# A two-stage mixing and SoLU kernel: an earlier transform, another form of the last unit, and other queues for its transfers

## The chip, the cores and the metric

The kernel runs on one core of one Trainium2 chip. The metric is the device time of one execution in microseconds (us). Five engines work side by side, each through its own list of instructions in order: PE (matrix products), DVE (vector), ACT (scalar functions), POOL (general) and SP (it issues transfers only). Transfers that SP or ACT issue are called plain here; POOL can also issue indirect ones, in which a table of row numbers says where each row goes. "The clock" of the profile is the share of full speed that PE was granted.

## What is computed

```python
X = np.fft.fft(np.fft.fft(x, axis=1), axis=2).real     # x: (8, 3136, 256)
x = X.reshape(8 * 3136, 256)
h = x @ w_in                                           # (25088, 1024)
e = np.exp(h - h.max(-1, keepdims=True))
solu = h * e / (e.sum(-1, keepdims=True) + 1e-9)
mu, var = solu.mean(-1, keepdims=True), solu.var(-1, keepdims=True)
out = ((solu - mu) / np.sqrt(var + 1e-6) * g_ln) @ w_out   # (25088, 256)
```

A real part of a two-dimensional Fourier transform is followed by a feed-forward block with a softmax-weighted activation and a layer norm. Everything is float32.

## The kernel before, in words

The eight sequences are taken as four **pairs** (p = 0 to 3). The transform over the 3136 = 49 x 64 positions has two steps. The first (`transform1`, L176) works over 49; by symmetry only 25 of its outputs (k1 = 0 to 24) are needed. It goes through a pair in eight chunks c, two halves each, and its result passes through a scratch tensor `zd` in memory: `keep` (L215) writes it from SP, and `turn` (L218) reads it back on POOL in five parts. The second step (`transform2`, L226) gives 128 rows for one k1.

A **unit** is one pair and one k1: 100 units, number u = 25 p + k1. A unit with k1 > 0 also yields the mirrored output row block 49 - k1, so it has two **signs** (0 and 1), each a tile of 128 rows by 1024 features. Per unit: PE makes h (`up`, L259), DVE joins the halves (`even` L267, `join` L273), ACT exponentiates (`expo` L281), DVE multiplies (`product` L289), ACT takes sums of squares (`square` L296) and small statistics (`stats` L303), POOL takes a power (`power` L313). DVE then transposes in 32 by 32 blocks (`turn_both` L334), and transfers complete the transposition (`move_blocks` L358: 16 transfers, four source blocks i times four q). Two units form a **batch**, which has one tile `v` and one tile `uT`; the `uT` tile is used again two batches later.

The last product (2 x 128 rows by 1024, times `w_out`) comes five steps later. For two-signed units it takes the form of **seven block products** (`Down`, L403): POOL first makes four sums S0, S1, S3, S2 of blocks of `uT` (`sums`, L388), and PE then does seven products of four matmuls each, named in their order p1, p4, p5, p6, p2, p3, p7. ACT copies the first (`seed`, L425) and scales three intermediate results (`keep_p`, `keep_x`, `keep_c`), DVE ends the unit (`finish`, L455). p6 waits for `seed`, p3 for `keep_p`, p7 for `keep_x`. Other units use the plain form (`down`, L462, and `scale`, L471).

`store` (L475) writes a unit's rows: sign 0 by a plain transfer from SP, sign 1 by an indirect transfer from POOL with the row numbers in `idx`. Each indirect store waits until the one before it is complete.

**What sets the order.** It is written out by hand (L671), in one loop over steps i (L828 to L901). Step i takes unit i through its activation, unit i - 5 through its last product, and stores unit i - 6; POOL makes the sums for unit i - 4. The blocks of a batch are moved by SP in every even step (L876). The last batch, units 98 and 99, is moved apart from the others, in steps 100 and 101 (L897 to L901). The transform of the next pair runs inside the same steps: `SUMS` (L639) gives the step in which each chunk begins. At a = i - SUMS: a = 0 and 1 is the POOL sum of the mirrored halves (`add_mirror`, L128), a = 1 and 2 the fold on DVE and ACT, a = 3 and 4 the two halves of `transform1`, and at a = 2 the chunk two places on is loaded (`load`, L109: `xa` from SP, `xb` from POOL). `turn_parts` (L665) reads pair p's scratch at steps 25 p - 4, - 3, + 2, + 6 and + 11.

Every plain transfer, whichever engine issues it, raises one of eight counters, which are handed out in turn over SP and ACT together; before a transfer is issued, its counter has to show that its former user is complete.

Of the kernel before, what the change touches and what calls it, by code (L numbers as in the profile page):

```python
# [20 lines left out]
N1, N2 = 49, 64  # L21
NK = N1 // 2 + 1
# [4 lines left out]
NC = NH // CH  # L27
# [8 lines left out]
def kernel(  # L36
# [19 lines left out]
    nc = tc.nc  # L56
    B, S, D = x.shape
# [3 lines left out]
    NP = B // 2  # L61
# [35 lines left out]
    def result(i):  # L97

        return banks[i % 4]
# [159 lines left out]
    def up(t, c):  # L259

        ps = ps_h.tile([P, FF], FP32, tag=f"h{c}", name=f"ps_h{c}")
        for half in range(2):
            fs = slice(half * HW, (half + 1) * HW)
            nc.tensor.matmul(ps[:, fs], t.q[:, c * P : (c + 1) * P], Wi[:, c, fs], start=True, stop=True)  # L264
        return ps

    def even(t, ps):  # L267

        t.ev = fpool.tile([P, FF], FP32, tag="ev", name="ev", bufs=1)
        nc.vector.scalar_tensor_tensor(out=t.ev, in0=w_mid, scalar=t.r, in1=ps,  # L270
                                       op0=ALU.mult, op1=ALU.add)
# [24 lines left out]
    def square(t, s):  # L296

        if s == 0:
            t.ssq = small.tile([P, 2], FP32, tag="ssq", name="ssq")
        nc.scalar.activation(out=t.h[s], in_=t.u[s], func=ACT.Square, bias=t.usum[:, s : s + 1], scale=-float(FF),  # L300
                             accum_out=t.ssq[:, s : s + 1])

    def stats(t):  # L303

        n = slice(0, len(t.signs))
        es2, v = (small.tile([P, 2], FP32, tag=tag, name=tag) for tag in ("es2", "v"))
        nc.scalar.activation(out=es2[:, n], in_=t.esum[:, n], func=ACT.Square, bias=limits[:, 3:4], scale=1e-3)
        for s in t.signs:
            nc.scalar.activation(out=v[:, s : s + 1], in_=t.ssq[:, s : s + 1], func=ACT.Identity, bias=es2[:, s : s + 1],  # L309
                                 scale=float(FF) ** -3)  # L310
        t.v = v
# [46 lines left out]
    def move_blocks(batch, units, engines=(nc.sync,)):  # L358

        v = batch.v[:, units].rearrange("p w (c q n) s -> p q (w c) (n s)", q=4, n=32)  # L360
        uT = batch.uT[:, units].rearrange("p w c i m -> p i (w c) m")
        for i in range(4):
            for q in range(4):
                a, b = slice(32 * i, 32 * i + 32), slice(32 * q, 32 * q + 32)
                engines[i % len(engines)].dma_start(out=uT[b, i], in_=v[a, q])
# [22 lines left out]
    def sums(t, prv):  # L388

        A11, A12, A21, A22 = blocks(t)  # L390
        S = blocks_of(t)
        for j, a, b, op in ((0, A21, A22, ALU.add), (1, S[0], A11, ALU.subtract), (3, A12, S[1], ALU.subtract),
                            (2, A11, A21, ALU.subtract)):
            i = nc.gpsimd.tensor_tensor(out=S[j], in0=a, in1=b, op=op)  # L394
            if j == 0 and prv:
                behind(i, prv)
# [65 lines left out]
    def down(t, s, ps=None):  # L462

        uT = t.batch.uT[:, t.w].rearrange("p c i (n s) -> p c (i n) s", s=2)
        if ps is None:
            ps = result(1)[:, 0:D]
        for c in range(KF):
            nc.tensor.matmul(ps, uT[:, c, :, s], Wo[:, c, :], start=(c == 0), stop=(c == KF - 1))
        return ps

    def scale(t, s, ps):  # L471
        t.ot[s] = fpool.tile([P, D], FP32, tag="ot", name="ot", bufs=6)
        nc.scalar.mul(out=t.ot[s], in_=ps, mul=t.rs[:, s : s + 1])

    def store(t, s):  # L475

        if s:
            i = NP * NC + t.p * (NK - 1) + t.k1 - 1
            dma = nc.gpsimd.indirect_dma_start(  # L479
                out=out, out_offset=bass.IndirectOffsetOnAxis(ap=idx[:, i : i + 1], axis=0),  # L480
                in_=t.ot[s], in_offset=None)
        else:
            dma = nc.sync.dma_start(out=out_k[t.p, t.k1], in_=t.ot[s])

        tc.declare_no_dep(dma.ins, group=f"out{1 - s}", reason="other rows of the output")
        tc.add_to_no_dep_group(f"out{s}", dma.ins)

# [146 lines left out]

    SUMS = [None] + [[f + 2 * c for c in range(NC)] for f in (3, 28, 53)]  # L639

    def ahead(pr, i, work):

        for c in range(NC):
            a = i - SUMS[pr.p][c]
            if work == "load" and (i == (pr.p - 1) * NK and c < 2 or a == 2 and c + 2 < NC):
# [12 lines left out]
    def ahead_pe(pr, i):  # L658

        for c in range(NC):  # L660
            half = i - SUMS[pr.p][c] - 3
            if half in (0, 1):
# [8 lines left out]
    with tc.manual_schedule():  # L671
# [71 lines left out]
        units = [Unit(p, k1) for p in range(NP) for k1 in range(NK)]  # L743
# [10 lines left out]
        def second_transform(i):  # L754
            if i < len(units):
                t = units[i]
                take2(t, transform2(pairs[t.p], t.k1))
                spread(t)

        def enter(i):  # L760
            cur = units[i]
            if i % 2 == 0:
                batches.append(Batch(i >= whole))
            cur.batch, cur.w = batches[-1], i % 2
# [9 lines left out]
        def other_pairs(i, do, *a):  # L774
            cur = units[i]
            if cur.p + 1 < NP:
                do(pairs[cur.p + 1], i, *a)

        batches = []
        begin(0)  # L780
        for i in range(whole + 1):
            cur = units[i]
            prv = units[i - 1] if i else None
# [36 lines left out]

        def by_seven(i):

            return 0 <= i < len(units) - 1 and len(units[i].signs) == 2

# [1 line left out]
        for i in range(whole + 1, len(units) + lag + 1):  # L828
            cur = units[i] if i < len(units) else None
            prv = units[i - 1] if whole < i - 1 < len(units) else None  # L830
            old = units[i - lag] if i < len(units) + lag else None
            seven = by_seven(i - lag)
            kept = units[i - lag - 1] if i >= lag + 1 else None

            if kept:
                store(kept, 0)
            if cur:
                enter(i)
                even(cur, up(cur, 0))
                cur.odd = up(cur, 1)  # L840
                second_transform(i + 2)
            if seven:
                new = Down(old, fresh)
                fresh = False
                new.p1()
                new.seed()
            if prv:
                stats(prv)
            if seven:
                new.p4()  # L850
                new.p5()
                new.keep_p()
            elif old:
                plain = [(s, down(old, s, result(s + 1)[:, 0:D])) for s in old.signs]
            if cur:
                other_pairs(i, ahead_pe)
            if seven:
                new.p6()
                new.keep_x()
                new.p2()  # L860
                new.keep_c()
            elif old:
                for s, ps in plain:
                    scale(old, s, ps)
            if cur:
                for s in cur.signs:
                    join(cur, s)
            if seven:
                new.p3()
                new.p7()  # L870
                new.finish()
            if cur:
                other_pairs(i, ahead, "mirror")
            if by_seven(i + 1 - lag):
                sums(units[i + 1 - lag], prv)
            if i % 2 == 0 and whole < i - 1 < len(units) - 2:  # L876
                batches[i // 2 - 1].place()
                move_blocks(batches[i // 2 - 1], slice(0, 2))
            if prv:
                power(prv)  # L880
            if kept and 1 in kept.signs:
                store(kept, 1)
            if cur:
                other_pairs(i, ahead, "fold")
                for s in cur.signs:
                    expo(cur, s)
                for s in cur.signs:
                    product(cur, s)
                for s in cur.signs:
                    square(cur, s)  # L890
                turn_both(cur)
                if cur.p == 0 and i in (5, 8, 11):
                    turn(first, (i + 1) // 3)
                for pr in pairs[1:]:
                    turn_parts(pr, i - pr.p * NK)
                other_pairs(i, ahead, "load")
            if i in (len(units), len(units) + 1):  # L897
                w = i - len(units)
                if w == 0:
                    batches[-1].place()  # L900
                move_blocks(batches[-1], slice(w, w + 1), (nc.sync, nc.gpsimd) if w else (nc.sync,))  # L901


def _tables(B, S, D):
# [73 lines left out]
```

## Time and profile before

| what | us |
|---|---|
| median of three runs | 1170.49 (1167.22 to 1172.64) |
| the profiled execution, its own time | 1172.88 |
| its span, first to last instruction | 1171.0 |
| PE busy | 1115.0 (95%) |
| DVE busy | 1022.6 (87%) |
| POOL busy | 868.2 (74%) |
| ACT busy | 757.5 (65%) |
| mean granted clock | 0.993 |

The profile gives busy times by engine and by source line, who waited for whom, and a timeline with start, length and, in brackets, the idle time before an instruction and what ended it. `L394 POOL ... S<-uT` means line 394 on POOL, writing S from uT; x16 means that 16 records are merged in one row. In a row of SP or POOL that issues transfers the length is that of issuing, not of moving the data. One float32 matmul has two records.

### The profile page before, as it was taken

The page shows a single profiled execution, that of the slowest core. Times are in us where ns is not written, and L with a number is a line of the kernel's source. Part 1 is how long each engine was busy: PE and PEld are TensorE (multiplying, and loading weights), DVE is VectorE, ACT ScalarE, POOL GpSimd, SP SyncE. Part 2 cuts the span into 40 slices and gives each one's busy share as a digit, 9 for nine tenths or more (in the row PEclk, how much of TensorE's full clock was granted, in tenths as well). Part 3 has the DMA queues.
Part 4 walks back from the last instruction along what each step waited for, and adds up shares of the span by engine and source line. Part 5 has one row for each costly group of instructions (what it writes and reads, how often), then busy time and mean ns, then how long its engine had stood idle before and what let it go on. Part 6 is the DMA issues. An engine that isn't in the chain of part 4 may idle for free. (4 is left out here: it accounts for less than half of the span.)

```text
span 1171.0 us, 21594 instructions
## 1 busy us (share of the span) xinstructions
PE 1115.0 (95%) x7002; PEld 891.1 (76%) x7002; DVE 1022.6 (87%) x1428; ACT 757.5 (65%) x1721; POOL 868.2 (74%) x750
## 2 busy tenths in 40 slices
PE   2987999999999999999999999999999999999996
PEld 1555787787787777778878777878878788888886
DVE  7889989888999989999899999888898998998860
ACT  4566666667666666667666766676666666666651
POOL 3035888874998797887688889876598687777675
PEclk9999999999999989999999999999999999999998
DMA  9672798866897969886869797976596675956653
GB/s 240 197 190 45 168 186 186 196 144 145 157 182 155 186 149 174 170 174 143 161 133 202 156 190 164 205 174 144 134 168 154 130 161 113 165 120 134 137 120 93
DMA packets 458479, 185.75 MB, mean 159 GB/s; under 512 B 425750, under 2 KB 440350, under 8 KB 458368
## 3 DMA queue, kind: packets, MB, share of 16 engines
q1 hardware_dynamic: 444608, 146.22, 60.9%
q0 software_dynamic: 13760, 38.16, 12.5%
q8 instruction: 57, 0.93, 0.3%
q14 instruction: 54, 0.44, 0.1%
HBM read 44.78 MB, written 38.80 MB: 71 GB/s over the span
## 5 line engine op out<-in xcount | busy, mean ns | idle before, releaser
L264 PE MATMUL ps_h<-Wi,q 128*128 128x512 f32 x800 | 363.6, 596 | 11.4 <-DVE ev L270 5.9
L394 POOL TENSOR_TENSOR S<-uT 128x512 f32<-128x512 f32 x190 | 258.4, 1360 | 102.1 <-DMA r<-q 39.2
L300 ACT ACTIVATE h<-u,usum 128x1024 f32<-128x1024 f32 x196 | 225.2, 1149 | 155.8 <-DVE u L293 155.8
L401 PE MATMUL ps_m<-Ws,S 128*128 128x128 f32 x2280 | 297.3, 277 | 5.7 <-POOL S L394 3.3
L401 PEld LDWEIGHTS ps_m<-Ws,S 128*128 128x128 f32 x2280 | 280.0, 193 | 10.1 <-POOL S L394 3.7
L264 PEld LDWEIGHTS ps_h<-Wi,q 128*128 128x128 f32 x800 | 144.3, 191 | 160.0 <-issue 141.7
L293 DVE SCALAR_TENSOR_TENSOR u<-h,u 128x1024 f32<-128x1024 f32 x196 | 261.0, 1367 | 0.4 <-ACT u L286 0.3
L286 ACT ACTIVATE u<-h,nmax 128x1024 f32<-128x1024 f32 x196 | 223.7, 1143 | 19.3 <-DVE nmax L278 14.6
L336 DVE STREAM_TRANSPOSE v<-u 128x2048 f32<-128x2048 f32 x93 | 215.4, 2316 | 3.2
L401 PE MATMUL ps_m<-Wo,uT 128*128 128x128 f32 x1520 | 210.9, 282 | 0.0
L401 PEld LDWEIGHTS ps_m<-Wo,uT 128*128 128x128 f32 x1520 | 195.2, 197 | 0.9 <-issue 0.9
L394 POOL TENSOR_TENSOR S<-uT,S 128x512 f32<-128x512 f32 x95 | 134.9, 1420 | 7.4
L278 DVE CUSTOM_DVE_ANT_0 h<-ev,ps_h 128x1024 f32<-128x1024 f32 x100 | 122.1, 1221 | 18.1 <-DVE ev L270 7.4
L479 POOL DMA_INDIRECT out_dram<-ot,idx x96 | 115.6, 1204 | 29.4 <-issue 19.1
L394 POOL TENSOR_TENSOR S<-S,uT 128x512 f32<-128x512 f32 x95 | 129.1, 1359 | 7.5
L278 DVE CUSTOM_DVE_ANT_0 h<-h,ps_h 128x1024 f32<-128x1024 f32 x96 | 117.2, 1221 | 14.2 <-DVE nmax L278 0.5
L270 DVE SCALAR_TENSOR_TENSOR ev<-w_mid,r,ps_h 128x1024 f32<-128x1024 f32 x100 | 124.0, 1240 | 4.1 <-ACT S L530 2.6
L316 POOL TENSOR_TENSOR rs<-v,neg_half 128x2 f32<-128x2 f32 (+1 forms) x100 | 85.8, 858 | 32.3 <-ACT v L309 27.0
L401 PE MATMUL ps_m<-Ws,uT 128*128 128x128 f32 x760 | 105.0, 281 | 0.0
L208 PE MATMUL ps_m<-y,F 98*100 98x258 f32 (+3 forms) x288 | 73.8, 392 | 30.4 <-DVE y L154 23.1
L401 PE MATMUL ps_m<-Wo,S 128*128 128x128 f32 x760 | 100.9, 276 | 0.0
L236 PEld LDWEIGHTS ps_m<-T,g 128*128 128x128 f32 x400 | 60.2, 191 | 48.8 <-issue 46.0
(92 smaller groups left out, 1175.8 us busy)
## 6 DMA issues: line engine op xcount, KB each, us to landing
uT<-v SPq DMA_DIRECT2D x752, 128.0 KB
out_dram<-ot SPq DMA_DIRECT2D x100, 128.0 KB
g<-zd POOLq DMA_DIRECT2D x72, 160.0 KB, 5.2
xa<-in_x_dram SPq DMA_DIRECT2D x28, 392.0 KB
zd<-z SPq DMA_DIRECT2D x24, 400.0 KB
raw_in<-in_moe_w_in_dram SPq DMA_DIRECT2D x4, 512.0 KB
raw_out<-in_moe_w_out_dram SPq DMA_DIRECT2D x2, 1024.0 KB
r<-q SPq DMA_DIRECT2D x100, 0.5 KB
```

The lines of the kernel that those rows point to most:

```text
L208: nc.tensor.matmul(o[..., cs], F[:, 2 * t + h, :], i[..., cs], start=first, stop=True, skip_group_check=True)
L264: nc.tensor.matmul(ps[:, fs], t.q[:, c * P : (c + 1) * P], Wi[:, c, fs], start=True, stop=True)
L270: nc.vector.scalar_tensor_tensor(out=t.ev, in0=w_mid, scalar=t.r, in1=ps, op0=ALU.mult, op1=ALU.add)
L278: nc.vector.tensor_tensor_reduce(out=t.h[s], in0=t.h[0] if s else t.ev, in1=t.odd, scale=1.0 if s else -0.5, scalar=3.0e38, op0=ALU.add, o ...
L286: nc.scalar.activation(out=t.u[s], in_=t.h[s], func=ACT.Exp, bias=t.nmax[:, s : s + 1], scale=-1.0, accum_out=t.esum[:, s : s + 1])
L293: t.last = nc.vector.scalar_tensor_tensor(out=t.u[s], in0=t.h[s], scalar=-1.0, in1=t.u[s], op0=ALU.mult, op1=ALU.mult, accum_out=t.usum[:, ...
L300: nc.scalar.activation(out=t.h[s], in_=t.u[s], func=ACT.Square, bias=t.usum[:, s : s + 1], scale=-float(FF), accum_out=t.ssq[:, s : s + 1])
L316: nc.gpsimd.tensor_tensor(out=t.rs[:, n], in0=t.v[:, n], in1=neg_half[:, n], op=ALU.pow)
L336: nc.vector.transpose(out=t.batch.v[:, t.w].rearrange("p f o -> p o f"), in_=t.both)
L394: i = nc.gpsimd.tensor_tensor(out=S[j], in0=a, in1=b, op=op)
L401: nc.tensor.matmul(o, a[:, c], b[:, c], start=start and c == 0, stop=c == n - 1, skip_group_check=True)
L479: dma = nc.gpsimd.indirect_dma_start(out=out, out_offset=bass.IndirectOffsetOnAxis(ap=idx[:, i : i + 1], axis=0), in_=t.ot[s], in_offset=None)
```

## The change

1. `SUMS`: the first chunk of the third pair (p = 2) begins in step 27 instead of 28; every load, sum, fold, `transform1` and write of the scratch of that pair comes one step sooner. The steps of `turn_parts` stay.
2. `by_seven` includes unit 99, so that the last unit too goes through POOL's sums and the seven block products.
3. The squares of unit 99 move from step 99 to step 100, behind `seed` of unit 95 on ACT.
4. In steps 100 and 101, the transfers of the last batch are issued 12 by SP and 4 by ACT in each; before it was 16 by SP in step 100, and 8 by SP and 8 by POOL in step 101.
5. Sign 1 of units 98 and 99 is stored by a plain transfer from ACT, with the rows addressed backwards, instead of indirectly by POOL. These stores are declared independent of the others.

```diff
     def store(t, s):
-        if s:
+        late = t.p == NP - 1 and t.k1 >= NK - 2
+        if s and late:
+            dma = nc.scalar.dma_start(
+                out=out.rearrange("(b k2 k1) d -> k1 b k2 d", b=B, k1=N1)[N1 - t.k1, 2 * t.p : 2 * t.p + 2, ::-1, :],
+                in_=t.ot[s])
+            tc.declare_no_dep(dma.ins, group="out1", reason="other rows of the output")
+        elif s:
             i = NP * NC + t.p * (NK - 1) + t.k1 - 1
             dma = nc.gpsimd.indirect_dma_start(
...
-        tc.declare_no_dep(dma.ins, group=f"out{1 - s}", reason="other rows of the output")
-        tc.add_to_no_dep_group(f"out{s}", dma.ins)
+        for group in ("out0",) if s else ("out1", "late1"):
+            tc.declare_no_dep(dma.ins, group=group, reason="other rows of the output")
+        tc.add_to_no_dep_group("late1" if s and late else f"out{s}", dma.ins)
...
-    SUMS = [None] + [[f + 2 * c for c in range(NC)] for f in (3, 28, 53)]
+    SUMS = [None] + [[f + 2 * c for c in range(NC)] for f in (3, 27, 53)]
...
         def by_seven(i):
-            return 0 <= i < len(units) - 1 and len(units[i].signs) == 2
+            return 0 <= i < len(units) and len(units[i].signs) == 2
...
                 new.seed()
+            if i == len(units):
+                for s in prv.signs:
+                    square(prv, s)
             if prv:
                 stats(prv)
...
-                for s in cur.signs:
-                    square(cur, s)
+                if i < len(units) - 1:
+                    for s in cur.signs:
+                        square(cur, s)
...
-                move_blocks(batches[-1], slice(w, w + 1), (nc.sync, nc.gpsimd) if w else (nc.sync,))
+                move_blocks(batches[-1], slice(w, w + 1), (nc.sync, nc.sync, nc.sync, nc.scalar))
```

## The prediction, as put on record before the changed kernel ran

> **What bounds the kernel now.** I read first the page's busy times, then the table by stretches, cut where `even` (L270) of units 25, 50 and 75 starts on DVE, so that each middle row is one pair of 25 units.
>
> ```profile
> PE 1115.0 (95%) x7002; PEld 891.1 (76%) x7002; DVE 1022.6 (87%) x1428; ACT 757.5 (65%) x1721; POOL 868.2 (74%) x750
> ...
> 325.74:606.24 280.50, 273.16 (x1734) 220.42 (x1734) 257.06 (x346) 183.57 (x427) 226.12 (x190) 0.99 0.80 165
> 606.24:878.62 272.38, 269.66 (x1734) 217.63 (x1734) 247.48 (x347) 183.90 (x427) 221.80 (x190) 1.00 0.80 169
> ```
>
> PE is the bound overall. But units 25 to 49, during which the third pair is transformed, take 280.50 us and units 50 to 74 take 272.38, with the same 1734 matmul records. The 8.1 us are waits. POOL's waits in the first of these stretches show them:
>
> ```profile
> POOL xa L134 <- DMA xa<-in_x_dram: 10.1, 3, 5.5
> POOL S L394 <- DMA r<-q: 7.9, 1, 7.9
> POOL xa L134 <- DVE ot L457: 6.4, 1, 6.4
> ...
> POOL xa L134 <- DMA zd<-z: 3.0, 1, 3.0
> ```
>
> POOL stands before the sums of mirrored halves (L134) for 10.1 + 6.4 + 3.0 = 19.5 us, all of it for loads (the DVE named in the third row had long been done). For the next pair no wait of L134 for a transfer is over 0.4. The timeline of SP says why: with an even first step the load of `xa` is queued in the same step as the 16 block moves, behind them.
>
> ```profile
> 428.19 13.31 SPq L365 DMA_DIRECT2D uT<-v  x16
> 441.61 0.75 SPq L117 DMA_DIRECT2D xa<-in_x_dram  x1
> ...
> 447.49 1.26 POOL L134 TENSOR_TENSOR xa<-xa,xb 98x510 f32<-98x510 f32 x1 [5.50 <-DMA xa<-in_x_dram]
> ```
>
> The load issued at 441.61 is wanted at once and comes 5.9 us later. In the fourth pair (first step 53, odd) a load issued at 708.92 is used at 721.00, 12.1 us later, without a wait.
>
> Then the end, by the timeline of all engines:
>
> ```profile
> 1114.57 13.81 SPq L365 DMA_DIRECT2D uT<-v  x16
> 1132.59 11.32 SPq L365 DMA_DIRECT2D uT<-v  x16
> 1144.59 7.52 SPq L365 DMA_DIRECT2D uT<-v  x8
> 1145.43 4.71 POOL L365 DMA_DIRECT2D uT<-v  x8
> 1150.15 1.51 POOL L394 TENSOR_TENSOR S<-uT 128x512 f32<-128x512 f32 x1
> 1151.71 3.44 PE L401 MATMUL ps_m<-Ws,S 128*128 128x128 f32 x16 [2.72 <-POOL S L394]
> 1157.72 7.08 PE L468 MATMUL ps_m<-Wo,uT 128*128 128x256 f32 x32
> 1160.68 0.98 POOL L479 DMA_INDIRECT out_dram<-ot,idx  x1 [4.08 <-DMA out_dram<-ot,idx]
> 1167.12 0.96 POOL L479 DMA_INDIRECT out_dram<-ot,idx  x1 [2.18 <-issue]
> ```
>
> The first row is the batch of units 96 and 97, the second unit 98, the next two unit 99. POOL issues eight moves, only then makes the sums of unit 98 (1150.15), PE waits 2.72, unit 99 follows in plain form, and the indirect stores come one after the other to 1168.1; the span ends at 1171.0.
>
> **What the Trainium skill says.** "DMA: Bandwidth & Descriptors", section "Issuing engines are not separate DMA queues": transfers of all issuing engines share the same 16 DMA engines, and a second issuer only saves issue time. The trace agrees: SP alone issued 16 single-unit moves at 11.32 / 16 = 0.71 us each, beside POOL at 7.52 / 8 = 0.94. "Perfetto Trace Analysis", section "DMA Instruction — HWDGE (DVE, Sync)": the semaphore wait lies ahead of the reported start, and the movement after the reported end. It agrees: the last move of batch 96/97 was issued by 1128.38, and the sums that need it started at 1131.85. "TensorE: Matmul & The Clock Gate", section "What's actually happening": after an idle window PE runs at half rate until it has been busy for about as long. It agrees roughly: after the 2.72 us wait, 16 records took 3.44 instead of the 1.95 at 1136.03.
>
> **Part 1, one step sooner.** Nothing is added or removed; eight loads on SP and POOL, 16 sums, folds, half transforms and eight scratch writes move by one step, past one set of moves, stores and sums each. Steps become odd, as in the fourth pair: each load stands ahead of the next even step's moves. The first two loads stay in step 25, which leaves the first sum two steps instead of three; they were issued at 332.46, and the sum comes after 347, so that is covered. If 280.50 becomes 272.4 the gain is 8.1. The scratch is also complete a step before `turn` reads it in step 46, which the fourth pair doesn't have; its 7.9 us wait for block moves (second fence, second row) may shrink. Bounds: 2 (the waits go, but PE finds another) to 12. I take **-8.5**.
>
> **Part 2, squares later.** Two squares of 1.15 leave the place ahead of `seed` of unit 95. Seed ran at 1130.10, and PE waited 1.57 for it. Now seed follows p1 at about 1127.3, p6 runs at 1128.8, p2 ends at 1130.8. But squares and statistics stand ahead of `keep_p` as before (1131.0), so p3 starts at 1131.6 instead of 1132.36, and `keep_c` ends at about 1132.2. Worth 0.7 locally, and swallowed by what follows.
>
> **Part 3, ACT's transfers.** This decides the end. I followed the built list of the changed kernel, transfer by transfer, with the counter each raises and waits for. Counters are handed out in an order in which ACT's four moves of unit 98 stand between the fifth and tenth of SP's 16 moves of batch 96/97. So **SP's tenth move of that batch waits for ACT's first move of unit 98**; the eleventh, 13th and 14th wait for ACT's other three. ACT issues these only behind `keep_c` of unit 95. SP reached its tenth move at 1114.57 + 9 x 0.86 = 1122.3; ACT gets there at 1132.2. Behind the waiting SP stand seven moves, the stores of units 93 and 94 and all of unit 98; for them wait POOL's sums and PE's p1 of unit 96.
>
> - No ACT transfer is in this trace. I take SP's issue of 0.62 (median of such moves) and the shortest landing that the trace gives for one, 2.7 from issue (longest 3.9; with POOL's reads in the way, up to 6.5: issue ended at 582.28, use 588.78). So ACT's first lands at 1134.9.
> - SP's last seven moves at 0.8 on average (between 0.71 and 0.86), the last landing 3 later: 1134.9 + 6 x 0.8 + 3 = 1142.7. PE had p1 of unit 96 at 1134.14 before: **+8.6 here**, 9 us of idle PE, and a slow clock after, +1.5 as above.
> - Then p1 to p2 of unit 96: 5 x 0.914 + 1.5 = 6.1 (a unit's seven products took 6.40: p1 of unit 96 at 1134.14, of unit 97 at 1140.54), `keep_c` 0.6, and only now ACT's first move of unit 99, for which in the same way SP's tenth move of unit 98 waits: landed at 1142.7 + 6.7 + 2.7 = 1152.1.
> - SP then issues three moves, a store and twelve moves: 2.1 + 0.55 + 11 x 0.71 = 10.5, and the last lands 3 later: 1165.6. PE's own chain (1142.7 + 1.5 + 3 x 6.4 = 1163.4) and POOL's (four sums 5.2 and a store 1.1 per unit: about 1163) are near it.
> - Last unit, 6.4 of PE: 1172.0.
>
> **Part 4, last unit in block products.** PE 6.4 for 7.08, -0.7. POOL gets four sums (1.5 + 1.3 + 1.3 + 1.0); S0 is ready 1.5 after landing, when p1 and p4 take 1.9, and the others keep ahead, so they are hidden.
>
> **Part 5, plain stores.** Before: POOL's chained indirect stores; from the end of PE's work (1164.8) to the end of the span 6.2. After: DVE 0.5, issue and landing 1.6 (SP's last store at 1161.93 landed near 1163.5), closing 1.1 (by estimate from the last landing to 1171.0): 3.3. So -2.9. If ACT's reversed addressing costs something, up to 1 more.
>
> End: 1172.0 + 3.3 = 1175.3, that is **+4.3** against 1171.0; bounds 0 (landings of 2.2, no slow clock) to +18 (each landing 6.5).
>
> **Sum.** -8.5 + 4.3 = -4.2. The profiled execution, 1172.88, would become 1168.7; it lies 2.4 above the median of the runs, so against 1170.49 I forecast 1166.3. About 0.5%, or 5.9 us, is what measurement can tell from no change.
>
> **Rivals.**
> - *The queue wait isn't met.* If SP isn't held, moves of unit 98 start at 1130.8, unit 99 lands at about 1153, PE ends at 1161 and the span at 1165: -6, with part 1 -14.5: 1156. For it: all else in the end section is shortened. Against: the counters of the built list. Chance 0.17.
> - *Part 1 only moves the stall.* Gain 2: 1170.5 - 2 + 4.3 = 1172.8. For it: the fourth pair still loses time at its turn (POOL waited 8.4 there) and PE is 97% busy. Against: the same parity gave 272.38. Chance 0.18.
> - *Slower:* the hold of SP costs its upper bound. It is met four times (ACT lands, SP's rest lands, again for unit 99). At 6.5 instead of about 2.9 each, 4 x 3.6 = 14.4 more: 1166.3 + 14.4 = 1180.7. From +2.5 each on the result is slower by over 0.5%, and without part 1's gain from +0.4 each. For it: these landings exist beside POOL's reads. Against: the end has little other traffic. Chance 0.13.
> - *The forecast:* 0.52, by itself 1161 to 1172.
>
> **Chances and range.** Faster by over 0.5% (under 1164.6): the first rival and a quarter of the forecast, 0.17 + 0.13 = 0.30. Slower: 0.13 and a little of the second rival, 0.14. Within: 0.56. For 8 in 10 the range runs from 1158 to 1177.
>
> **What would show it.** Units 25 to 49 near 272 us and no POOL wait for `xa` there over 1 us: part 1. A gap of some 10 us on SP within the 16 moves of batch 96/97, followed by PE idle for 6 to 10 us before p1 of unit 96 and a clock dip: part 3. L401 in place of L468 at the very end, and no indirect store after unit 97. The prediction is wrong if SP issues those 16 moves in one go, or if the stretch of the third pair doesn't shrink.

## The result, and the profile after

The changed kernel takes 1175.87 us (median of 15 runs, 1172.66 to 1179.04) against 1171.57 of the kernel before (15 runs on the same chip): ratio 1.0036, 95% interval 1.0020 to 1.0052. It is a little slower, where the forecast was a little faster. Its profiled execution took 1176.30 us, the span 1174.5 (before: 1172.88 and 1171.0).

Cut at the same places as before, where `even` (L270) of a unit starts on DVE, the two profiles compare like this (us):

| stretch | before | after | difference |
|---|---|---|---|
| start of unit 0 | 59.45 | 62.23 | +2.8 |
| units 0 to 24 | 266.29 | 265.31 | -1.0 |
| units 25 to 49 | 280.50 | 273.36 | -7.1 |
| units 50 to 74 | 272.38 | 271.68 | -0.7 |
| units 75 to 98 | 242.73 | 242.49 | -0.2 |
| unit 99 to the end of PE's work | 43.45 | 50.71 | +7.3 |
| end of PE's work to the end of the span | 6.20 | 8.72 | +2.5 |

The first row isn't the change: the start of unit 0 lay between 58.5 and 63.0 in the kernels below, whose instructions up to there are the same.

The table by stretches of the changed kernel has these rows for the third and the fourth pair (us; busy time and records of PE, PEld, DVE, ACT, POOL; clock; share of the DMA engines; GB/s):

```profile
327.54:600.90 273.36, 270.44 (x1734) 219.10 (x1734) 245.14 (x346) 183.52 (x427) 218.98 (x190) 0.99 0.80 169
600.90:872.58 271.68, 269.65 (x1734) 217.62 (x1734) 247.35 (x347) 183.96 (x427) 221.74 (x190) 1.00 0.81 169
```

The two pairs now take nearly the same. Of POOL's waits in the first of them, these are the ones to set beside those of before:

```profile
POOL xa L134 <- DVE u L293: 11.2, 10, 2.7
...
POOL S L394 <- DVE ot L457: 7.7, 1, 7.7
...
POOL xa L134 <- DMA out_dram<-ot: 2.7, 1, 2.7
```

No wait of L134 for the load of `xa` is over 0.4 us now. The 11.2 us are ten waits behind DVE, the longest 2.7; the 2.7 us of the third row lie before the sum at 511.46, whose load had been issued 22 us earlier, at 489.17. But the one long wait of the sums (L394), which ended at 588.78 before, is still there with 7.7 us.

Now the end. The timeline of the changed kernel (start, length, instructions; in brackets the idle time before and what ended it):

```profile
1108.27 24.27 SPq L365 DMA_DIRECT2D uT<-v  x16
...
1124.68 0.74 ACTq L365 DMA_DIRECT2D uT<-v  x1
1125.46 1.94 ACTq L365 DMA_DIRECT2D uT<-v  x3
...
1134.29 12.67 SPq L365 DMA_DIRECT2D uT<-v  x12
...
1135.82 2.05 PE L401 MATMUL ps_m<-Wo,uT 128*128 128x128 f32 x8 [8.71 <-DMA out_dram<-ot]
1135.84 1.49 POOL L394 TENSOR_TENSOR S<-uT 128x512 f32<-128x512 f32 x1 [15.72 <-DMA out_dram<-ot]
...
1142.74 2.61 ACTq L365 DMA_DIRECT2D uT<-v  x4
...
1147.64 7.79 SPq L365 DMA_DIRECT2D uT<-v  x12
...
1158.96 1.18 PE L401 MATMUL ps_m<-Wo,uT 128*128 128x128 f32 x8 [1.68 <-DMA uT<-v]
```

The 16 moves of the batch of units 96 and 97 took SP 13.81 us before, 24.27 now: SP stands still in the middle of them. By the single records it issues the ninth at 1115.06 and the tenth only at 1126.97, 2.3 us after ACT has begun to issue its first move (1124.68), whose counter the tenth waits for. PE and POOL wait for the last of them, 8.71 and 15.72 us (the store named as releaser had come just before; the moves are what was late). After it PE's first eight records take 2.05 where 1.11 is usual. SP's own list of waits in this part says the same in one row:

```profile
SPq L365 <- DMA uT<-v: 15.7, 3, 11.3
SPq L984 <- DMA out_dram<-ot: 7.3, 3, 3.1
```

The second row belongs to the end. L984 is the closing section of the program; there SP waits three times for stores, 7.3 us in all (before: 5.8 us for an indirect store of POOL and 1.2 for one of its own). The transfers of the last 11 us (1164 to 1175, in 40 slices of 0.275 us: the busy tenths of the 16 DMA engines and the rate; then the issues with their size and the median time to landing) show which:

```profile
DMA  0000011101555883111111011111111110000000
GB/s 0 0 0 0 0 30 45 45 30 41 78 112 186 287 305 123 60 48 34 7 7 7 11 30 48 48 48 48 48 45 52 45 37 0 0 0 0 0 0 0
...
out_dram<-ot ACTq DMA_DIRECT2D x2, 128.0 KB
out_dram<-ot SPq DMA_DIRECT2D x1, 128.0 KB
out_dram<-ot,idx POOLq DMA_INDIRECT x1, 5.0
```

POOL's and SP's stores make the peak of 305 GB/s. By the records of its queue, ACT's first mirrored store moves data from 1165.4 to 1168.7, beside them, and its second from 1169.2 to 1173.1, mostly alone: 45 to 48 GB/s in most slices, with the engines busy for a tenth. The last data lands at 1173.1, 7.3 us after PE's last product (1165.78). The Trainium skill, "DMA: Bandwidth & Descriptors", section "Why a DMA increments its semaphore by 16 and not by 1", gives a reason: a transfer is spread over the largest number up to 16 that divides the slowest dimension of both sides. The backward store addresses 2 x 64 x 256 elements, so that is 2. The trace agrees: from 1169.5 to 1173.0 the mean share of the engines is 0.12, and 2 of 16 is 0.125.

And something else ends at the same moment. In the list of the closing section, POOL's row (count; shortest, median, longest in ns; start of the first and the last), first of the changed kernel, then of the kernel before:

```profile
L984 POOLq DRAIN  x3: 46/102/11245, 1162.4 to 1174.3; - x3
```

```profile
L973 POOLq DRAIN  x3: 46/102/3338, 1166.9 to 1170.8; - x3
```

DRAIN is an instruction that POOL carries out in the closing section, called its drain here. The longest of its three starts at 1162.4 and is done at 1162.4 + 11.245 = 1173.65. POOL's last real instruction, an indirect store of 0.99 us at 1164.36, was over at 1165.35: the drain takes 8.3 us more. Before, POOL's last store was over at 1168.08, the drain at 1166.9 + 3.338 = 1170.24, 2.2 us later. So two things hold the end, the stores on two engines and POOL's drain. The experiments take them apart.

### The profile page after: what moved, and what is told of

It reads as the page before. It is cut to its first block, busy times and chain, and to the rows that moved or that the text cites. A ratio compares the mean times of both kernels' runs of the same rounds, so it can differ in the third digit from the quotient of the medians.

```text
span 1174.5 us, 21661 instructions
## 1 busy us (share of the span) xinstructions
PE 1113.4 (95%) x7026; PEld 891.7 (76%) x7026; DVE 1010.2 (86%) x1430; ACT 758.6 (65%) x1723; POOL 859.2 (73%) x744
## 4 chain that ended last, share of the span: by engine, by line
PE 86%; DMA 5%; DVE 4%; SPq 2%; issue 1%; ACT 1%; POOL 1%; ACTq 0%; DVEq 0%; POOLq 0%
PE ps_m L401 50%; PE ps_h L264 27%; PE ps_m L208 4%; PE ps_m L236 3%; DMA room<-in_x_dram 2%; SPq L365 1%; DVE h L278 1%; DMA F<-in_f_tab_dram 1%; DMA uT<-v 1%; SPq L216 1%; DVE u L293 1%; PE ps_m L468 1%; PE wps L608 1%; ACT h L300 1%; DMA r<-q 1%
## 5 line engine op out<-in xcount | busy, mean ns | idle before, releaser
L394 POOL TENSOR_TENSOR S<-uT 128x512 f32<-128x512 f32 x192 | 262.2, 1365 | 118.7 <-DMA out_dram<-ot 46.4
L401 PE MATMUL ps_m<-Wo,uT 128*128 128x128 f32 x1536 | 214.1, 283 | 10.4 <-DMA out_dram<-ot 8.7
L401 PEld LDWEIGHTS ps_m<-Wo,uT 128*128 128x128 f32 x1536 | 197.9, 198 | 11.7 <-issue 11.7
L394 POOL TENSOR_TENSOR S<-uT,S 128x512 f32<-128x512 f32 x96 | 137.2, 1429 | 7.5
L394 POOL TENSOR_TENSOR S<-S,uT 128x512 f32<-128x512 f32 x96 | 130.3, 1358 | 7.5
L270 DVE SCALAR_TENSOR_TENSOR ev<-w_mid,r,ps_h 128x1024 f32<-128x1024 f32 x100 | 124.0, 1240 | 2.4 <-ACT S L537 2.3
L485 POOL DMA_INDIRECT out_dram<-ot,idx x94 | 107.8, 1147 | 22.9 <-issue 16.5
L316 POOL TENSOR_TENSOR rs<-v,neg_half 128x2 f32<-128x2 f32 (+1 forms) x100 | 79.2, 792 | 30.9 <-ACT v L309 25.6
L401 PEld LDWEIGHTS ps_m<-Ws,uT 128*128 128x128 f32 x768 | 98.8, 198 | 0.0
```

Source lines behind the costliest of these rows:

```text
L316: nc.gpsimd.tensor_tensor(out=t.rs[:, n], in0=t.v[:, n], in1=neg_half[:, n], op=ALU.pow)
L401: nc.tensor.matmul(o, a[:, c], b[:, c], start=start and c == 0, stop=c == n - 1, skip_group_check=True)
L485: dma = nc.gpsimd.indirect_dma_start(out=out, out_offset=bass.IndirectOffsetOnAxis(ap=idx[:, i : i + 1], axis=0), in_=t.ot[s], in_offset=None)
```

## The experiments

Theories. *Hold:* the +7.3 before PE's end is SP's wait for ACT's moves, as forecast. *Two engines:* the +2.5 behind PE's end comes from the backward stores, each of which only two DMA engines carry. *Drain:* it comes from POOL's closing drain, and then the question is what makes that long. The changed kernel is "after" in what follows, and the diffs show only the lines that matter; all ratios are against the kernel before, in runs on the same chip.

**1. After, with all late moves by SP.**

```diff
-move_blocks(batches[-1], slice(w, w + 1), (nc.sync, nc.sync, nc.sync, nc.scalar))
+move_blocks(batches[-1], slice(w, w + 1), (nc.sync,))
```

> The changed kernel with all 32 moves of the last batch issued by SP; nothing else differs. Theory (SP is held at its tenth move of batch 96/97 by the counter of a transfer that ACT issues much later): those 16 moves are issued without a gap in about 14 us (24.3 in the changed kernel), PE's wait of 8.7 us before unit 96 goes, and from `even` of unit 99 to the end of PE's work it takes 41 to 44 us instead of 50.7; the whole is 6 to 9 us faster than the changed kernel, some 3 us faster than before. Rival (the last unit's block products, with POOL's four sums, and the squares behind `seed` are what lengthens the end): the stretch stays at 48 us or more.

Measured: 1167.7 us, ratio 0.9957 (0.9939 to 0.9975). Its timeline:

```profile
1106.72 13.09 SPq L365 DMA_DIRECT2D uT<-v  x16
...
1122.94 11.05 SPq L365 DMA_DIRECT2D uT<-v  x16
```

SP goes through its 16 moves without a stop, and from unit 99 to PE's end it is 41.16 us in place of 50.71. The hold is shown. The end doesn't shorten: 8.8 us behind PE's last product, drain included.

**2 and 3. After, with the stores of ACT forward.** In the first the rows are addressed forward, in the second each store is also cut into two transfers of 64 rows; in both, the mirrored rows of units 98 and 99 land in the opposite order.

```diff
-    ...[N1 - t.k1, 2 * t.p : 2 * t.p + 2, ::-1, :], in_=t.ot[s])
+    ...[N1 - t.k1, 2 * t.p : 2 * t.p + 2, :, :], in_=t.ot[s])
```

> The changed kernel with the two ACT stores writing their rows forwards instead of backwards (the mirrored rows of units 98 and 99 stand in the wrong order in the output; the work is equal). Theory (the stores are slow because the memory side's outermost dimension counts 2, so that only two of the 16 DMA engines carry them): no change, from PE's end to the end of the span 8 to 9 us as in the changed kernel (8.7). Rival (addressing backwards is slow): 3.5 to 5 us.

> As the kernel with forward rows, but each of the two stores is issued as two transfers of 64 rows, so that the outermost dimension counts 64 instead of 2 (the mirrored rows of units 98 and 99 stand in the wrong order). Theory of the two engines: from PE's end to the end of the span 3.5 to 5 us instead of 8.7, the DMA share in the last stretch no longer near 2/16, and the whole 4 to 5 us faster than the changed kernel. Rival (transfers on ACT's queue land late whatever their shape): still 7 us or more.

Measured: 1175.38 us in a single execution of the first; 1175.1 us, ratio 1.0030 (1.0018 to 1.0041), for the second. In the second, SP waits only 2.8 us for stores in the closing section, in five waits. Then it waits 4.6 us more, under the name of PE, until POOL's drain is over; and the drain is as long as in the changed kernel:

```profile
SPq L987 <- PEq L987: 5.1, 2, 4.6
SPq L987 <- DMA out_dram<-ot: 2.8, 5, 1.1
```

```profile
L987 POOLq DRAIN  x3: 46/102/11243, 1162.8 to 1174.6; - x3
```

So the two engines alone are not what holds the end; making the stores fast gains nothing, because the drain ends at 1174.0 here.

The first of the two was meant as a test of the direction, with the stores still on two engines. It isn't one: forward rows are one run of 128, so it also changed the number of engines. The forecast of 8 to 9 us came true (8.7) by luck, since the drain held the end. But the records of its transfers settle the question of the direction. A row of 1 KB takes 46 ns in the median, backwards in the changed kernel and forwards here. On two engines 64 rows follow each other, 64 x 46 ns = 2.9 us of the 3.3 to 3.9 that a store took there; spread, each of ACT's two stores took 0.52 us here (about 250 GB/s). So the number of engines made the stores slow, and not the direction.

**4. After, moves by SP, unit 99's mirrored rows by POOL again.**

```diff
-late = t.p == NP - 1 and t.k1 >= NK - 2
+late = t.p == NP - 1 and t.k1 == NK - 2
...
-move_blocks(batches[-1], slice(w, w + 1), (nc.sync, nc.sync, nc.sync, nc.scalar))
+move_blocks(batches[-1], slice(w, w + 1), (nc.sync,))
```

> All moves of the last batch by SP, and of the two ACT stores only unit 98's is kept, which has time to land; unit 99's is an indirect store from POOL again, which waits for unit 97's alone. Theory: both losses of the end go; from `even` of unit 99 to PE's end 41 to 44 us, from PE's end to the end of the span 5 to 6 us; with the third pair's 7 us this is 8 to 11 us faster than before, ratio 0.991 to 0.993. Rival (the third pair's gain is given back at the end whatever its queues, because PE is near its bound): not more than 4 us faster than before.

Measured: 1170.84 us, ratio 0.9996 (0.9983 to 1.0009). PE ends at 1155.0 as in the first run, POOL's last store is over at 1157.24, the drain at 1165.7, 8.4 us behind it, and the span ends 11.4 us behind PE's end, where 5 to 6 were expected. The drain follows POOL's last instruction, so a later instruction costs its delay in full. Against the first run unit 99's plain store is worth 3 us, but not by its own speed: it ends POOL's work sooner.

**5. Before, with ACT's moves alone.**

```diff
-(nc.sync, nc.gpsimd) if w else (nc.sync,))
+(nc.sync, nc.sync, nc.sync, nc.scalar))
```

> The kernel before with one part of the change alone: the moves of the last three units by SP, SP, SP and ACT in place of SP and POOL. Hold theory: SP's tenth move waits for ACT's first move of unit 98, so the instruction stream ends some 7 us later on TensorE (about 1172 us in place of 1164.8), ratio about 1.006 if TensorE's end and the span's end stay 6.2 us apart. If the short closing drain of the kernel before (3.3 us) hung on POOL's own moves of blocks, the drain here is some 8.3 us behind POOL's last indirect store and the distance grows to about 12 us: ratio about 1.011. If moves by ACT cost nothing: ratio 0.999 to 1.001.

Measured: 1186.41 us, ratio 1.0130 (1.0104 to 1.0156): the case with the long drain. PE's end comes 8.6 us later (52.06 from unit 99 on, against 43.45), and the end behind it is 11.1 instead of 6.2, though all mirrored stores are indirect as before. Third part, both effects: about 13.5 us in the profile. POOL's drain:

```profile
L973 POOLq DRAIN  x3: 46/102/9682, 1172.3 to 1182.5; - x3
```

It is over at 1182.0, 8.5 us behind POOL's last store, against 2.2 before. The only thing taken from POOL is its eight moves.

**6. After, moves by SP, all mirrored stores by POOL.**

```diff
-late = t.p == NP - 1 and t.k1 >= NK - 2
+late = t.p == NP - 1 and t.k1 >= NK
...
-move_blocks(batches[-1], slice(w, w + 1), (nc.sync, nc.sync, nc.sync, nc.scalar))
+move_blocks(batches[-1], slice(w, w + 1), (nc.sync,))
```

> The changed kernel with its moves by SP and all mirrored rows by indirect DMA from POOL again, as before. Theory that POOL's closing drain ends 8.3 us behind its last indirect store wherever that stands: last store issued about 4 us behind TensorE's end (1155), drain until about 1167 to 1168, ratio about 1.000. Rival, that the drain is long only in kernels with plain stores by ACT: TensorE's end to the span's end as before, 6.2 us, so span about 1161, ratio about 0.993 to 0.994, and then the plain stores cost 2.5 us.

Measured: 1172.52 us, ratio 1.0009 (0.9990 to 1.0027). The drain is long (8.5 us) without any plain store by ACT; the rival falls. From PE's end to the span's end it is 15.2 us. The plain stores (first run: 8.8) thus save 6.4 us where the drain is long, since they take POOL's chained last stores away.

**7 and 8. After, moves by SP, unit 97's mirrored store plain as well; and the same with transfers of 64 forward rows.**

```diff
-late = t.p == NP - 1 and t.k1 >= NK - 2
+late = t.p == NP - 1 and t.k1 >= NK - 3
...
-move_blocks(batches[-1], slice(w, w + 1), (nc.sync, nc.sync, nc.sync, nc.scalar))
+move_blocks(batches[-1], slice(w, w + 1), (nc.sync,))
```

> The changed kernel with its moves by SP and with the mirrored rows of unit 97 by plain DMA from ACT too, so that POOL's last indirect store is that of unit 96. Theory that the drain ends 8.3 us behind the last indirect store: POOL is done soon after its last sum (about 1154 us), and the end is set by the plain stores at 48 GB/s on two engines: span 1161 to 1163, ratio 0.993 to 0.9955. Rival, that the drain ends 9.4 us behind POOL's last sum: drain until 1162.7, ratio 0.9957 as with the moves by SP alone.

> As the kernel with three plain mirrored stores, but each store in two forward transfers of 64 rows (so the rows of the last three mirrored units land in the wrong order), which spread over the engines. Theory that the drain hangs on the last indirect store: both holds of the end are gone, the span ends 3.5 to 5 us behind TensorE's end, at 1158.5 to 1160, ratio 0.991 to 0.9925. Rival, that the drain follows the last sum by 9.4 us: 1162.7, ratio 0.9957.

Measured: 1173.38 us, ratio 1.0017 (1.0006 to 1.0029), and 1169.20 us, ratio 0.9976 (0.9963 to 0.9988). Neither theory had these times. The timeline of the first shows why:

```profile
1139.01 15.91 SPq L365 DMA_DIRECT2D uT<-v  x16
...
1147.21 1.14 ACTq L479 DMA_DIRECT2D out_dram<-ot  x1
...
1156.68 2.05 PE L401 MATMUL ps_m<-Wo,uT 128*128 128x128 f32 x8 [7.78 <-DMA uT<-v]
```

The store at 1147.21 stands among SP's 16 moves of unit 99. The thirteenth of these waits for the counter that this store raises: SP was done with the twelfth at 1146.80 and issues the thirteenth at 1152.38. It is the hold of part three again, by a store this time. (In the second PE waits 5.62 us at this place.) On the drain both agree: POOL's last indirect store ended more than 20 us before the drain did, and the drain still ends 8.3 us behind POOL's last *sum*. So it follows POOL's last instruction of any kind; the theory of the last indirect store falls.

**9. Before, with the third pair one step sooner, alone.**

```diff
-for f in (3, 28, 53)
+for f in (3, 27, 53)
```

> The kernel before with one part of the change alone: the third pair's first transform one step sooner. Theory from the stretch of units 25 to 50 in the changed kernel (280.5 to 273.4 us): about -7 us and no other change, ratio 0.993 to 0.995. Rival, that the gain came from the other parts, or is given back in the stretch behind: ratio 0.999 to 1.001.

Measured: 1166.80 us, ratio 0.9948 (0.9931 to 0.9966), that is -6.1 us (-8.1 to -4.0). Units 25 to 49 take 273.08 us. POOL's moves are as before here, and so is its drain (2.2 us).

**10 and 11. After without part three (moves by SP and POOL as before); and the same with forward stores of 64 rows.**

```diff
-(nc.sync, nc.sync, nc.sync, nc.scalar))
+(nc.sync, nc.gpsimd) if w else (nc.sync,))
```

> The changed kernel with the moves of the last three units as before (by SP and POOL), that is the change without its third part. Theory that POOL's own moves shorten its closing drain: TensorE ends near 1157, the drain is done some 2 us behind POOL's last instruction, and the end is set by the two stores on two engines each, 6.5 to 8 us behind TensorE's end: span 1163.5 to 1165, ratio 0.994 to 0.996. Rival, that the drain takes 8.3 us behind POOL's last instruction wherever the stores are plain: span 1165 to 1167, ratio 0.996 to 0.9975; the length of the drain in the trace tells them apart.

> As the changed kernel with the moves as before, but each late mirrored store in two forward transfers of 64 rows (so the mirrored rows of units 98 and 99 land in the wrong order), which spread over the engines. Theory that POOL's own moves shorten the drain: both holds of the end are gone, the span ends 3.5 to 4.5 us behind TensorE's end: span 1160.5 to 1162, ratio 0.991 to 0.9935. Rival (drain of 8.3 us all the same): 8.7 us behind TensorE's end, span 1165 to 1166.5, ratio 0.9955 to 0.997.

Measured: 1168.04 us, ratio 0.9968 (0.9955 to 0.9981), and 1162.40 us, ratio 0.9917 (0.9897 to 0.9936). The drain of the first:

```profile
L984 POOLq DRAIN  x3: 46/102/4990, 1155.8 to 1168.4; - x3
```

It is over at 1160.8, 2.1 us behind POOL's last instruction. Yet the span ends 8.35 us behind PE's end, as in the changed kernel. Here it is the two engines (1158 to 1170, slices of 0.3 us):

```profile
GB/s 0 0 0 0 314 123 20 34 48 24 41 27 61 119 287 61 55 58 38 7 27 27 48 48 48 48 48 48 48 27 14 0 0 0 0 0 0 0 0 0
```

The last data lands at 1158 + 31 x 0.3 = 1167.3, about 7 us behind PE's end. With the stores spread as well, both are gone, and the span ends 4.2 us behind PE's end.

**12. After with all moves by SP but four of unit 98's by POOL, and forward stores of 64 rows.** (The expectation calls them moves of unit 97; the edit is to step 100, in which unit 98 is moved.)

```diff
...
-(nc.sync, nc.sync, nc.sync, nc.scalar))
+(nc.sync,) if w else (nc.sync, nc.sync, nc.sync, nc.gpsimd))
```

> The changed kernel with all moves by SP but four of unit 97's, which POOL issues, and the late mirrored stores in two forward transfers each (mirrored rows of units 98 and 99 in the wrong order). Theory that a few late direct moves by POOL shorten its closing drain, whatever their number: drain done about 2 us behind POOL's last instruction, the span ends 3.5 to 4.5 us behind TensorE's end, 1159 to 1161, ratio 0.990 to 0.993. Rival, that the drain's length goes with the number of POOL's transfers in the whole program (206 here, 202 in the changed kernel, 212 before): drain still 8 us or more, 8.7 us behind TensorE's end, ratio about 0.9955.

Measured: 1163.11 us, ratio 0.9924 (0.9901 to 0.9947). Four moves are enough. POOL issues them some 20 us before the end of its work, which comes at 1156.16, and its drain is over 2.3 us behind that:

```profile
1133.77 2.42 POOL L365 DMA_DIRECT2D uT<-v  x4
...
L987 POOLq DRAIN  x3: 46/102/5195, 1153.2 to 1160.8; - x3
```

The span ends 4.5 us behind PE's end.

**13. The same moves; unit 98's mirrored rows by ACT backwards, unit 99's indirect by POOL, every row in its place.**

```diff
-late = t.p == NP - 1 and t.k1 >= NK - 2
+late = t.p == NP - 1 and t.k1 == NK - 2
...
-(nc.sync, nc.sync, nc.sync, nc.scalar))
+(nc.sync,) if w else (nc.sync, nc.sync, nc.sync, nc.gpsimd))
```

> The changed kernel with three edits: all moves by SP but four of unit 97's, which POOL issues; the mirrored rows of unit 98 by plain DMA from ACT as in the change; those of unit 99 by indirect DMA from POOL as before. Theory that the end has two holds, POOL's long drain and the slow plain store, and that this lifts both with every row in its place: TensorE ends near 1155, POOL's last store is issued 2.3 us later and the drain ends some 2.3 us behind it: span 1159.5 to 1161, ratio 0.9905 to 0.993. Rival, that the short drain needs the plain stores or the moves of the last two units by POOL: the drain is 8.4 us behind POOL's last store, span 1165 to 1167, ratio 0.9985 to 1.0005.

Measured: 1166.12 us, ratio 0.9949 (0.9936 to 0.9962). The drain is short, 1.9 us behind the last store, but that store is late for a third reason:

```profile
1160.14 0.96 POOL L485 DMA_INDIRECT out_dram<-ot,idx  x1 [4.90 <-DMA out_dram<-ot,idx]
```

It waits for the landing of POOL's store before it, whose data (1156.8 to 1159.0) moves beside that of ACT's store (1155.3 to 1158.6). So the span ends 8.2 us behind PE's end, where 4.5 to 6 were expected.

**14. After with the third pair two steps sooner than before.**

```diff
-for f in (3, 27, 53)
+for f in (3, 26, 53)
```

> The changed kernel with the third pair's first transform yet one step sooner (26 in place of 27; before: 28). Theory that the gain of the stretch of units 25 to 50 comes from being sooner: stretch at or below 273.4 us, ratio 1.000 to 1.004 as the changed kernel or less. Rival, that it comes from the step's being odd, that is from which unit of a couple carries the loads: stretch near 280 us again, ratio 1.008 to 1.011.

Measured: 1192.14 us, ratio 1.0166 (1.0123 to 1.0208). Units 25 to 49 take 291.5 us. "Sooner is better" falls. With an even step the waits of before are back, and longer; POOL's in that stretch begin with

```profile
POOL xa L134 <- DMA xa<-in_x_dram: 10.7, 2, 7.5
```

The parity of the step may thus be part of it, with no other odd step tried; but 26 is also 11 us worse than 28, and no run says why.

**The ends side by side** (us; the last column is from PE's last product to the end of the span):

| kernel | late moves by | late mirrored stores | POOL's last instruction over | its drain over | between | end behind PE |
|---|---|---|---|---|---|---|
| before | SP, POOL | indirect | 1168.1 | 1170.2 | 2.2 | 6.2 |
| after | SP, ACT | two engines | 1165.4 | 1173.7 | 8.3 | 8.7 |
| 3 | SP, ACT | spread | 1165.7 | 1174.0 | 8.3 | 8.7 |
| 10 | SP, POOL | two engines | 1158.7 | 1160.8 | 2.1 | 8.4 |
| 11 | SP, POOL | spread | 1158.6 | 1160.6 | 2.1 | 4.2 |
| 12 | SP, four POOL | spread | 1156.2 | 1158.4 | 2.3 | 4.5 |
| 6 | SP | indirect | 1163.9 | 1172.4 | 8.5 | 15.2 |
| 5 | SP, ACT | indirect | 1173.5 | 1182.0 | 8.5 | 11.1 |

The second to the fifth kernel are the four combinations of a long or a short drain with slow or spread stores. Of these the end is short only where both are cured. Each cause alone is enough for all of the 8.4 to 8.7 us.

## Why the prediction was wrong, by its own steps

- *Part 1, -8.5.* Right in its mechanism, a little too large: -7.1 in the changed kernel, -7.4 alone in the profile, -6.1 (-8.1 to -4.0) in the runs. The waits for `xa` are gone as told. The part of the sum that failed is the extra on top of the next pair's level: the 7.9 us wait of the sums, which "may shrink", is 7.7, and the stretch stopped at 273.4, not at 272.0.
- *Part 2, swallowed, and part 4, -0.7.* Right where they act: the seven products of unit 95 take 7.3 us in run 10 and 8.2 in run 9, and unit 99 takes PE 6.6 and 7.1. At PE's end nothing of it is clear: with the same moves, from unit 99 on it is 43.17 and 43.92 us with both parts (runs 10 and 11) and 43.79 without (run 9). The two weren't tried apart.
- *Part 3, +7.2 before PE's end.* Right, in place and size: +7.3. SP's stop at the tenth move, PE's idle 8.71 us and the slow records after it are where they were forecast. The first rival (the queue isn't held) falls with it.
- *Part 5, -2.9 behind PE's end.* This is the step that failed: +2.5. It took the change at the end to be the removal of POOL's chained stores, and gave the backward store the landing of SP's forward one, 1.6 us, with "up to 1 more" for the addressing. (The direction itself costs nothing that the records show: 46 ns for a row both ways.) Two things were wrong. First, the shape: on two engines a store's data takes 3.3 to 3.9 us, the second comes behind the first, and its last data lands 7.3 us behind PE's end; that alone gives 8.4 (run 10). Second, "closing 1.1" was taken as fixed. It holds POOL's drain, which part three lengthens from 2.2 to about 8.3 us behind POOL's last instruction by taking the moves away from POOL; that alone gives 8.7 (run 3). Plain stores do save time where the drain is long, but the 2.9 of the forecast are not confirmed by that: between run 5 and the changed kernel, which differ in parts 1, 2 and 4 too, it is 11.1 to 8.7, and with the stores alone changed (runs 6 and 1) 15.2 to 8.8. With both cured the end is 4.2 (run 11), near the 3.3 that was forecast.
- *The sum.* The profile says +3.5 where -4.2 was forecast: 5.4 of the 7.7 us come from part 5, 1.4 from part 1, 1.8 from the start and units 0 to 24 (within the scatter of the runs), less the 0.9 by which units 50 to 98 ran faster. The rival that ended slower had another mechanism, landings of 6.5 us within the hold; it didn't come about, as the hold cost what was forecast.

What stays open: why a direct transfer issued by POOL shortens its drain. In the six kernels with a short drain the last one lay 15 to 28 us before the end of the drain, in the ten with a long one 172 us or more. Two other counts part the kernels in the same way, and no run separates them. Since its last direct transfer POOL had issued 2 to 4 indirect ones in the six and 16 to 19 in the ten; within the ten the distance grows with that number, from 8.26 us (16) to 8.49 (19). And POOL's transfers in the whole program are 206 to 212 in the six and 201 to 204 in the ten. That the length goes with this total (the rival of run 12) would need a step of 6 us between 204 and 206, which is unlikely but not excluded. Also not tried: two backward transfers of 64 rows each, which would keep every row in its place.

Among the kernels with every row in its place the best are run 9 (0.9948), run 13 (0.9949) and run 1 (0.9957), which these measurements don't tell apart.

## What to carry to other kernels

Before work is taken off an engine near the end of a program, look at what that engine does in the closing section: the time from the last product to the end is a maximum over stores and drains of all engines, not a constant. Where two things end together, curing one shows nothing; try them together and apart before either is dismissed. A transfer that goes to a second queue can hold the first one through the counters that they share (SP stood still for 11.3 us here), and a store's shape decides how many engines carry it (two or sixteen here).

## What the runs showed of the hardware that was not expected

- POOL's closing drain ended 8.3 to 8.5 us behind POOL's last instruction in the ten kernels in which POOL's last direct transfer lay 172 us or more before the end of the drain, and 1.9 to 2.3 us behind it in the six in which that transfer lay within the last 28 us (four such transfers were enough).
- A store of 128 KB with the shape 2 x 64 x 256 took 3.3 to 3.9 us for its data (34 to 40 GB/s on the whole), at 46 ns in the median for a row of 1 KB. As 128 forward rows it took 0.52 us, with the same 46 ns for a row. In two transfers of 64 rows each half took 0.46 us (run 11), and the end came 4 us sooner where nothing else held it (8.4 and 4.2 us behind PE's end).
